# Output projection by seven products on pairs of row blocks, with its weights and first pair prepared inside attention

## The chip, the core and the metric

One core of a Trainium2 chip runs the whole kernel. The metric is device time in microseconds (us); the median of three runs before the change is 849.94 us (849.49 to 851.43).

## What is computed

A gate mixes a Fourier layer and a windowed attention layer, both of the same `x` (2048 rows, 512 columns):

```python
g = _sigmoid((x * gate_w).sum(-1, keepdims=True))
a = x @ dft_hid_re.T;  b = x @ dft_hid_im.T
A = dft_seq_re @ a - dft_seq_im @ b            # 2048 x 2048 matrices
q, k, v = split(x @ wqkv)                       # 32 heads of 16, 256 back
o = softmax(mask(q @ k.T * Dh ** -0.5)) @ v
return g * A + (1 - g) * (o @ wo)
```

(This is cut and reordered from the reference; every matrix is fp32.) The change concerns `o @ wo`, the output projection: 2048 x 512 by 512 x 512, scaled by `1 - g` (`g0` in the kernel) and added to the rest.

## The kernel before, in words

Every product is made of three matmuls: each fp32 operand is split into a rounded part `hi` and a rest `lo`, and `TERMS` lists hi.hi, hi.lo and lo.hi. A split is a cast (`hi`) and a subtraction on DVE (`lo`). So each operand that comes from memory costs a cast and a subtraction before TensorE can use it.

Attention runs over 128 steps (4 groups of heads `g`, 32 blocks of 64 keys). The loop at L864 issues for step `n` the scores `s` (`s_pair`, L366) and, 19 steps later (`LAG`; `k = n - 19`), the transposed scores `t` (`t_pair`, L448), whose exponentials ACT writes to `pt` or `home` (L449) and GpSimd (POOL) masks (L453, L457). Every six steps the products with `v` follow in one run (`pv`, L474), from two value tiles `vpad` that are used in turn. A step needs a "pad" of its queries or keys (`make_pad`, L349 on DVE and L347 on ACT), made one step ahead in one of two buffers. `ring0` and `ring1` hold the queries and keys of a group. A finished piece of `o` is scaled (`o_out`, L495) and stored to `o_scr`.

Between these matmuls `fill` draws dense ones from the generator `dense` (L594), one matmul at a time: the projections, and then the 2048 x 2048 products of the Fourier layer (`c_part`, L528, output `dc`). Their stationary operand comes in pieces (`raw<-ci`, 128 x 1024), loaded two ahead into two buffers and split into one of three `hi`/`lo` buffers: a cast and a subtraction for each half, on DVE (`split_soon`, L115). Each row block of 128 rows takes two pieces of 24 matmuls of 512 columns.

When attention is over, about 8 pieces of the dense work are left. `attention_done` (L779) then reuses `ring0` and `ring1`: it loads `wo` in two halves, splits them on DVE into `fin`, and marks the tail as begun (`FIN`). From then `c_part` calls `tail_step` (L766) at every fourth chunk of three matmuls. A tail step takes up to two row blocks that were prepared three steps before (`wo_block`, L803: 12 matmuls of 512 columns, L811, and one update on DVE, L813), and prepares others (`wo_prep`, L796: a load of `o` from `o_scr`, a cast on ACT and a subtraction on DVE). Row blocks whose Fourier part is finished wait in the list `wait`; blocks 14 and 15 are done ahead of it (`mixed`). The last row block ends the program: `c_final` (L543) makes its last two chunks in two halves of 256 columns (L558), so that the first half is stored (L561) while the second is computed.

The order on TensorE is that of the code. On DVE, ACT, POOL and SP a scheduler orders the instructions by a model of their times when the kernel is built, except where `behind` (L68) holds one after a marked one (`mark`, L64). Nearly all DMAs are issued by SP, in one queue; a DMA that waits there holds those behind it. The tiles `t` and `s` share four PSUM buffers (pool `ps_a`).

Of the kernel before, what the change touches and what calls it, by code (L numbers as in the profile page):

```python
# [7 lines left out]
F32 = mybir.dt.float32  # L8
F32R = mybir.dt.float32r
AF = mybir.ActivationFunctionType  # L10
OP = mybir.AluOpType
# [3 lines left out]
P = 128  # L15
S = 2048
D = 512
DK = D // P
NG = 4
NP = 4  # L20
BQ = 64
NB = S // BQ
WIN = 320
# [4 lines left out]
SWITCH = 6  # L28
# [4 lines left out]
def fnet_window_mix(ctx: ExitStack, tc: tile.TileContext, xT, x, wqk, wv, wr, wi, cr, ci, wo, gw, out):  # L33
    nc = tc.nc

    const = ctx.enter_context(tc.tile_pool(name="const", bufs=1))
# [18 lines left out]
    def ld(dst, src):  # L55
        mark("sp", nc.sync.dma_start(dst, src))  # L56

    def f(ap):
        return ap.bitcast(F32)
# [16 lines left out]
    masks = []  # L76

    def split(hi, lo, raw, act=False):
        if act:
            nc.scalar.copy(hi, raw)  # L80
# [4 lines left out]
        return nc.vector.tensor_sub(lo, raw, f(hi))  # L85
# [251 lines left out]
    def make_pad(i, n):  # L337
        if not 0 <= n < NG * NB:
            return
        t = pads[i][n % NPAD]  # L340
        b = n % NB
        with behind(*(("act", "dve") if n < NPAD else ("dve",) if i == 0 and n < 24 else ())):
            for h in range(2):
                src = f(ring[i][:96, :, b * BQ:(b + 1) * BQ])
                dst = turned(t)[:96, :, :, h] if i else t[:96, :, 64 * h:64 * h + 64]
                if i and h:
                    nc.scalar.activation(dst, src, AF.Copy, scale=half[:96, h:h + 1])  # L347
                else:
                    nc.vector.tensor_scalar(dst, src, half[:96, h:h + 1], None, op0=OP.mult)  # L349
        PAD[i, n] = t  # L350

    ML = {}
# [169 lines left out]

    def c_part(w, chunks, ab, ps, ends):
        for i in chunks:
            if FIN and i % 4 == 0:
                tail_step()
            for n, (a, b) in enumerate(TERMS):
                nc.tensor.matmul(ps, w[a][:, i % 8 * 128:i % 8 * 128 + 128], ab[SC[i]][:, b],  # L528
                                 start=i == ends[0] and a + b == 0, stop=i == ends[1] and a == 1)
                job(i % 8 * 3 + n + 1)  # L530
                if i != chunks[-1] or a == 0:
                    yield
# [10 lines left out]
    def c_final(get, ab):  # L543
        ps = ps_d.tile([P, 512], F32, name="dc", tag="d")
        g = g1[:, 15:16]
        for j in range(2):
            w = get((1, 30 + j))
            yield from c_part(w, range(16)[8 * j:8 * j + 8 - 2 * j], ab, ps, (0, 13))
            yield
        while wait:  # L550
            tail_step()
        r = mixed.pop(15)
        late(nc.vector.scalar_tensor_tensor, r, ps, g, r, OP.mult, OP.add)
        for c, dma in ((slice(0, 256), nc.sync), (slice(256, 512), nc.scalar)):
            ps2 = ps_a.tile([P, 512], F32, name="t", tag="st")
            for i in (14, 15):
                for a, b in TERMS:
                    nc.tensor.matmul(ps2[:, c], w[a][:, i % 8 * 128:i % 8 * 128 + 128], ab[SC[i]][:, b, c],  # L558
                                     start=i == 14 and a + b == 0, stop=i == 15 and a == 1)
            nc.vector.scalar_tensor_tensor(r[:, c], ps2[:, c], g, r[:, c], op0=OP.mult, op1=OP.add)  # L560
            dma.dma_start(out[15][:, c], r[:, c])  # L561
        yield
# [22 lines left out]
    def late(fn, *args):  # L585
        with behind("act", "dve"):
            return fn(*args)  # L587
# [172 lines left out]
    now = []  # L760
    wait = []
    mixed = {}
    born = {}
    clock = iter(range(99))

    def tail_step():  # L766
        t = next(clock)
        for tb in [tb for tb in O if born[tb] < t - 2][:2]:
            if tb in wait:
                wait.remove(tb)  # L770
                ld(out[tb], wo_block(tb, 1))
            else:
                mixed[tb] = wo_block(tb, 0)
        for tb in (*wait[:5], 15, 14, *wait[5:]):
            if tb not in O and tb not in mixed and len(O) < 7 and (tb > now[-1] or tb in wait):
                wo_prep(tb)
                born[tb] = t

    def attention_done():  # L779
        fin = const.tile([P, 8192], F32R, name="fin", tag="ring0")  # L780
        ORAW.extend(f(fin[:, 4112 + 512 * i:4624 + 512 * i]).rearrange("p (g t) -> p g t", g=NG) for i in range(7))
        fin = fin[:, 16:4112].rearrange("p (j c h e) -> p j c h e", j=2, c=2, h=2)
        OS.append(const.tile([P, 8, 2, NG, P], F32R, name="os", tag="ring1"))
        for j in range(2):
            raw = st.tile([P, 1024], F32, name="raw", bufs=2)
# [5 lines left out]
    OS = []  # L791
    ORAW = []
    O = {}
    slot = iter(range(99))

    def wo_prep(tb):  # L796
        oraw = ORAW[0]
        ORAW.append(ORAW.pop(0))
        ld(oraw, o_scr[tb // 4][:, :, tb % 4 * P:tb % 4 * P + P].rearrange("g p t -> p g t"))
        O[tb] = OS[0][:, next(slot) % 8]  # L800
        split(O[tb][:, 0], O[tb][:, 1], oraw[:], True)

    def wo_block(tb, half):  # L803
        o = O.pop(tb)
        r = ev.tile([P, 512], F32, name="ev")
        ld(r, r_scr[half if half or tb < 16 - SWITCH else 2][tb])
        ps = ps_a.tile([P, 512], F32, name="t", tag="st")
        n = 0
        for g in range(NG):
            for a, b in TERMS:  # L810
                nc.tensor.matmul(ps, o[:, a, g], FIN[0][:, g // 2, g % 2, b], start=n == 0, stop=n == 11)  # L811
                n += 1
        nc.vector.scalar_tensor_tensor(r, ps, g0[:, tb:tb + 1], r, op0=OP.mult, op1=OP.add)  # L813
        return r


    stream = dense()
# [39 lines left out]
    def v_next(n):  # L857
        if n < N:
            for c in range(2):
                need(("v", n % NB // 2 + c))  # L860
            with behind(*(("sp",) if n < 8 else ())):
                v_load(n)

    for n in range(N + LAG + 1):  # L864
        k = n - LAG
        if k == 0:
            masks.append(n)
        ring_ahead(n + 1)
        if k in (-1, 4):
            v_spread(0 if k < 0 else 4)  # L870
        if k in (-4, -1, 4):
            v_next({-4: 0, -1: 4, 4: 8}[k])
        if n == 0:
            make_pad(0, 0)
        for p in range(NP):
            if n < N:
                s_pair(n, p)
            fill(n)
            visit = p == 0 and (k - summed >= (6 if more else 4) or k == N)
            if 0 <= k < N and not visit:  # L880
                t_pair(k, p)
            if p == 0:
                make_pad(0, n + 1)
                if k >= -1:
                    make_pad(1, k + 1)
            fill(n)
            if visit:
                for j in range(summed, k):
                    pv(j)
                summed = k  # L890
                if k < N:
                    t_pair(k, p)
            for at_n, at_p, do in TURN if n > 12 else FIRST:
# [61 lines left out]
```

## Time and profile before

| | |
|---|---|
| median of three runs | 849.94 us |
| the profiled execution | 850.96 us |
| its span, first to last instruction | 849.0 us |
| TensorE's granted clock | 1.00 |
| PE busy, 5,166 matmuls | 843.7 us |
| DVE busy | 611.3 us |
| ACT busy | 593.6 us |
| POOL busy | 256.8 us |
| matmuls of the output projection (L811), 512 columns | 192 |

The page gives each engine's busy time and follows the chain of work that ended last. Busy matmuls overlap, so the mean duration of one (392 ns for L811) is not its pace; the pace is the distance between starts. Waits are put down to the instruction that released them. In the profile, "PEld" is the loading of a matmul's stationary operand, and "SPq" the issue of a DMA by SP.

### The profile page before, as it was taken

How to read it: one execution, taken by the hardware profiler on the slowest of the kernel's cores; microseconds unless marked ns; L12 is line 12 of the kernel's file. 1: busy time of each engine (PE TensorE's matmuls, PEld its weight loads, DVE VectorE, ACT ScalarE, POOL GpSimd, SP SyncE). 2: the span in 40 equal slices, each digit the busy share in tenths (PEclk: the TensorE clock that was granted, in tenths of full speed). 3: DMA queues.
4: the chain of work that ended last, by engine and by line, in shares of the span. 5: the costliest groups of instructions: out<-in, count | busy, mean ns of one | idle time of the engine just before them, and what ended most of it. 6: DMA issues, size and time to landing. Idle time of an engine off the chain costs nothing.

```text
span 849.0 us, 16711 instructions
## 1 busy us (share of the span) xinstructions
PE 843.7 (99%) x5166; PEld 691.4 (81%) x5166; DVE 611.3 (72%) x1999; ACT 593.6 (70%) x1798; POOL 256.8 (30%) x578
## 2 busy tenths in 40 slices
PE   9999999999999999999999999999999999999998
PEld 6888888888888788888888887888887878878887
DVE  5588978667978787787787886887987864437531
ACT  6488888878888897787877886877777865532100
POOL 8102332233332233342323333343233364620000
PEclk9999999999999999999999999999999999999999
DMA  8776678476765275533454557969774435339732
GB/s 296 244 228 186 214 243 257 181 233 225 216 222 178 63 211 134 171 115 123 137 158 127 177 150 227 308 216 306 254 215 134 138 121 164 128 118 333 225 134 75
DMA packets 94345, 160.99 MB, mean 190 GB/s; under 512 B 26800, under 2 KB 35760, under 8 KB 94256
## 3 DMA queue, kind: packets, MB, share of 16 engines
q1 hardware_dynamic: 93824, 159.28, 60.2%
q8 instruction: 40, 0.66, 0.3%
q10 hardware_dynamic: 432, 0.66, 0.2%
q14 instruction: 49, 0.40, 0.1%
HBM read 108.27 MB, written 51.64 MB: 188 GB/s over the span
## 4 chain that ended last, share of the span: by engine, by line
PE 94%; DMA 2%; DVE 2%; issue 1%; SPq 0%; ACT 0%; DVEq 0%; ACTq 0%
PE dc L528 39%; PE dqk L280 9%; PE dab L303 9%; PE t L448 9%; PE s L366 8%; PE o L474 8%; PE t L811 5%; PE dv L303 5%; DMA raw<-wo 1%; DMA ev<-l_scr 1%; PE s L268 1%; DVE sm L368 1%; PE dv L592 0%; SPq L56 0%; DVE pad L349 0%
## 5 line engine op out<-in xcount | busy, mean ns | idle before, releaser
L528 PE MATMUL dc<-big,hi 128*128 128x512 f32 x1020 | 344.5, 393 | 0.0
L371 ACT ACTIVATE sm<-sm,ml 128x320 f32<-128x320 f32 (+4 forms) x512 | 277.4, 543 | 59.6 <-DVE ml L368 54.1
L368 DVE CUSTOM_DVE_ANT_0 sm<-s,mask 128x320 f32<-128x320 f32 (+4 forms) x512 | 235.0, 464 | 108.6 <-PE s L366 73.2
L449 ACT ACTIVATE pt<-t 128x320 f32<-128x320 f32 (+4 forms) x392 | 159.8, 411 | 87.7 <-PE t L448 82.1
L528 PE MATMUL dc<-big,lo 128*128 128x512 f32 x510 | 200.3, 393 | 0.0
L528 PEld LDWEIGHTS dc<-big,hi 128*128 128x128 f32 x1020 | 180.4, 188 | 22.6
L448 PE MATMUL t<-ring,pad 128*128 128x320 f32 (+4 forms) x512 | 156.8, 306 | 0.1
L453 POOL TENSOR_SCALAR_AFFINE_SELECT pt<-pt 128x128 f32<-128x128 f32 x196 | 71.2, 363 | 283.3 <-ACT pt L449 279.7
L366 PE MATMUL s<-ring,pad 128*128 128x320 f32 (+4 forms) x512 | 155.3, 303 | 0.3 <-DVE ml L368 0.2
L349 DVE TENSOR_SCALAR pad<-ring,half 96x256 fp32r<-96x256 f32 x384 | 120.4, 360 | 11.9 <-PE t L448 11.7
L448 PEld LDWEIGHTS t<-ring,pad 128*128 128x128 f32 x512 | 96.1, 188 | 31.1 <-issue 8.7
L366 PEld LDWEIGHTS s<-ring,pad 128*128 128x128 f32 x512 | 96.2, 188 | 21.7 <-DVE ml L368 2.0
L528 PEld LDWEIGHTS dc<-big,lo 128*128 128x128 f32 x510 | 95.9, 188 | 11.9
L371 ACT ACTIVATION_READ_ACCUMULATOR sm<-sm,ml 128x1 f32 x512 | 97.4, 190 | 0.0
L587 DVE TENSOR_TENSOR lo<-raw,hi 128x512 fp32r<-128x512 f32 x137 | 93.8, 694 | 0.1
L303 PE MATMUL dab<-hi,big 128*128 128x512 f32 x256 | 89.0, 394 | 0.0
L280 PE MATMUL dqk<-big,hi 128*128 128x512 f32 x240 | 85.0, 393 | 0.0
L431 POOL TENSOR_SCALAR vpad<-vr,half 128x256 f32<-128x256 f32 x64 | 61.3, 969 | 65.3 <-PE o L474 30.3
L587 DVE CAST hi<-raw 128x512 fp32r<-128x512 f32 x137 | 57.7, 431 | 20.5 <-PE dc L528 17.0
L347 ACT ACTIVATE pad<-ring,half 96x256 fp32r<-96x256 f32 x128 | 66.8, 522 | 0.0
L457 POOL TENSOR_SCALAR_AFFINE_SELECT pt<-pt 128x128 f32<-128x128 f32 x172 | 60.8, 354 | 0.0
L474 PE MATMUL o<-pt,vpad 128*32 128x320 f32 (+4 forms) x1072 | 57.7, 351 | 0.0
(96 smaller groups left out, 912.5 us busy)
## 6 DMA issues: line engine op xcount, KB each, us to landing
qk_scr<-home SPq DMA_DIRECT2D x32, 512.0 KB
ring<-qk_scr SPq DMA_DIRECT2D x32, 512.0 KB
raw<-cr SPq DMA_DIRECT2D x32, 512.0 KB
raw<-ci SPq DMA_DIRECT2D x32, 512.0 KB
r_scr<-ev SPq DMA_DIRECT2D x42, 256.0 KB
ev<-r_scr SPq DMA_DIRECT2D x42, 256.0 KB
ab_scr<-home SPq DMA_DIRECT2D x20, 512.0 KB
big<-ab_scr SPq DMA_DIRECT2D x20, 512.0 KB
```

The costliest lines, as they stand in the source:

```text
L280: nc.tensor.matmul(ps, w[a][:, c:c + 128], XT[dk, ss][:, b], start=n == 0, stop=n == 11)
L303: nc.tensor.matmul(ps, XT[dk, ss][:, a, c * 128:(c + 1) * 128], wh[b], start=n == 0, stop=n == 11)
L349: nc.vector.tensor_scalar(dst, src, half[:96, h:h + 1], None, op0=OP.mult)
L366: nc.tensor.matmul(ps[:, :w], PAD[0, n][:, p], ring[1][:, p, k0:k0 + w], start=True, stop=True)
L368: mark("dve", nc.vector.tensor_tensor_reduce(out=sm[:, :w], in0=ps[:, :w], in1=mask[:, WIN - w:], scale=1.0, scalar=3e38, op0=OP.add, op1= ...
L371: mark("act", nc.scalar.activation(sm[:, :w], sm[:, :w], AF.Exp, bias=nm[:, c], scale=-1.0, accum_out=l[:, c]))
L448: nc.tensor.matmul(ps[:, :w], PAD[1, n][:, p], ring[0][:, p, q0:q0 + w], start=True, stop=True)
L449: nc.scalar.activation(pt[:, p, :w], ps[:, :w], AF.Exp, scale=-1.0)
L453: nc.gpsimd.affine_select(a, a, pattern=[[0, 2], [2, 64]], compare_op=OP.is_ge, fill=0.0, base=1, channel_multiplier=-1)
L474: nc.tensor.matmul(OT[g, sb][32 * p:32 * p + 32, q - sb * 512:e - sb * 512], v2[:, p], pt[:, p, q - q0:e - q0], start=first, stop=kb == 8 ...
L528: nc.tensor.matmul(ps, w[a][:, i % 8 * 128:i % 8 * 128 + 128], ab[SC[i]][:, b], start=i == ends[0] and a + b == 0, stop=i == ends[1] and a ...
L587: return fn(*args)
```

## The change

The row blocks are taken in pairs. With a pair's `o` as a matrix of two row blocks by two halves of the contraction (256 each), and `wo` as two halves by two halves of columns, Winograd's form of Strassen's method replaces eight products of quarter size by seven. Each is of 128 rows, 256 deep, 256 columns: two matmuls deep, three terms, six matmuls of 256 columns. It needs four sums of quarters of `o`, four of `wo`, and additions of the results.

- **Weights.** `wo` comes in two column halves into the tiles `pad0` (free after the last scores), in steps 110 and 116. DVE makes four differences of each (`wo_diffs`) and seven casts and seven subtractions (`fin_split`), block by block to step 121, into columns of `ring0` and `ring1` that the last group no longer reads.
- **First pair.** Its `o` is loaded in step 121, summed by DVE in step 123 (`first_sums`), cast by ACT and subtracted by DVE up to step 125. These DVE jobs stand behind the pad that was marked last.
- **Other pairs.** POOL makes the four sums (`wo_sums`), ACT casts and DVE subtracts (`wo_split`); tiles of the attention that has ended (`vpad`, `pad1`, `pad0`, `home`, `pt`) hold the data.
- **Products.** `tail_step` comes twice as often. A pair's first four products (24 matmuls) and the other three (18) are two steps apart, with 12 dense matmuls between; three of the last accumulate on the first ones in PSUM. DVE adds the results to the rows (`into`).
- **Raw pieces.** Behind the end of attention the cast of a dense piece goes to ACT.

```diff
-            jobs.append(lambda c=c: late((nc.vector if masks else nc.gpsimd).tensor_copy, hi[:, c], raw[:, c]))
+            jobs.append(lambda c=c: late(nc.scalar.copy if FIN else (nc.vector if masks else nc.gpsimd).tensor_copy,
+                                         hi[:, c], raw[:, c]))
...
-            if FIN and i % 4 == 0:
+            if FIN and i % 2 == 0:
                 tail_step()
...
-        for tb in [tb for tb in O if born[tb] < t - 2][:2]:
-            if tb in wait:
-                wait.remove(tb)
-                ld(out[tb], wo_block(tb, 1))
...
+        for i, begin in enumerate(BEGIN):
+            if t == begin + 2:
+                wo_end(i)
+            if t == begin:
+                wo_begin(i)
+            if i and t == max(1, begin - 3):
+                wo_split(i)
+            if i and t == max(0, begin - 6):
+                wo_sums(i)
+            if i > 3 and t == begin - 9:
+                wo_load(i)
+
+    BEGIN = range(2, 26, 3)
...
+    def wo_diffs(c):
+        b11, b12, b21, b22 = (q for t in RAW[c] for q in quarters(t, 2))
+        t1, t3, t2, t4 = spare()
+        for t, x, y in ((t1, b12, b11), (t3, b22, b12), (t2, b22, t1), (t4, b21, t2)):
+            nc.vector.tensor_sub(t, x, y)
+        DIFF[c] = b11, b21, b22, t4, t1, t2, t3
+
+    def fin_split(c, m):
+        split(fin(m, 0, c), fin(m, 1, c), DIFF[c][m])
 
     def attention_done():
-        fin = const.tile([P, 8192], F32R, name="fin", tag="ring0")
...
-            ld(raw, wo[j])
-            for c in range(2):
-                split(fin[:, j, c, 0], fin[:, j, c, 1], raw[:, c * 512:c * 512 + 512])
-        FIN.append(fin)
+        RT.append(const.tile([P, 6, 512], F32, name="rt", tag="home"))
...
+        r_load(0)
+        wo_load(1)
+        r_load(1)
+        for i in range(2, 4):
+            wo_load(i)
+        FIN.append(True)
...
+    def sums(eng, s1, s2, s3, s4, a, b):
+        eng.tensor_add(s1, b[:, :256], b[:, 256:])
+        eng.tensor_sub(s3, a[:, :256], b[:, :256])
+        eng.tensor_sub(s2, s1, a[:, :256])
+        eng.tensor_sub(s4, a[:, 256:], s2)
...
+    def wo_split(i):
+        if i > 1:
+            r_load(i)
+        split_a(i)
+        s = EX[i][:, :1024].rearrange("p (m t) -> p m t", m=4)
+        n = 3 if i % 2 else 4
+        split(*halves(spots(1, n, COL[i % 2])), s[:, :n], True)
+        if i % 2:
+            split(*halves(os_spot(6, 1)), s[:, 3], True)
...
+        def product(ps, m, n, start=True):
+            o = os_spot(m, i % 2).rearrange("p (h c t) -> p h c t", h=2, c=2)
+            for c in range(2):
+                for a, b in TERMS:
+                    nc.tensor.matmul(ps, o[:, a, c], fin(n, b, c), start=start and c == 0 and a + b == 0,
+                                     stop=c == 1 and a == 1, skip_group_check=True)
...
+        product(p1, 0, 0)
+        nc.scalar.copy(u, p1)
+        product(p6, 4, 5)
+        nc.vector.tensor_add(u2, p6, u)
+        product(p7, 5, 6)
+        into(r2[:, hi], p7, gb)
+        product(p5, 3, 4)
+        into(r2[:, hi], p5, gb)
+
+        def rest():
+            into(r1[:, hi], u2, ga)
+            product(p1, 1, 1, False)
+            into(r1[:, lo], p1, ga)
+            product(p7, 2, 3, False)
+            into(r2[:, lo], p7, gb)
+            product(p5, 6, 2, False)
+            into(r1[:, hi], p5, ga)
+            into(r2.rearrange("p (n e) -> p n e", n=2), u2.unsqueeze(1).to_broadcast([P, 2, 256]), gb)
...
+    BEFORE_END = {(121, 3): first_load, (123, 0): first_sums, (123, 2): lambda: split_a(0)}
+    for c, k in enumerate((113, 118)):
+        BEFORE_END[(110, 116)[c], 2] = lambda c=c: wo_fetch(c)
+        BEFORE_END[k - 1, 1 + 2 * c] = lambda c=c: wo_diffs(c)
+        for j, m in enumerate((0, 1, 2, 4, 6, 5, 3)):
+            BEFORE_END[k + j // 2, j % 2 * 2] = lambda c=c, m=m: fin_split(c, m)
+    for j, m in enumerate((3, 5, 4, 6)):
+        BEFORE_END[124 + j // 2, j % 2 * 2] = lambda m=m: first_split(m)
```

The change moves instructions on every engine; three places matter. In the rows, `dc` are the dense matmuls, and `ring_267`, `ring_268` are `ring0`, `ring1`; the changed file's lines are one or more higher (L529 for L528).

TensorE between two blocks of the output projection, before:

```order
L811 MATMUL t<-fin,os 128x512 x24
L528 MATMUL dc<-big,hi 128x512 x2
L528 MATMUL dc<-big,lo 128x512
L528 MATMUL dc<-big,hi 128x512 x2
L528 MATMUL dc<-big,lo 128x512
L528 MATMUL dc<-big,hi 128x512 x2
L528 MATMUL dc<-big,lo 128x512
L528 MATMUL dc<-big,hi 128x512 x2
L528 MATMUL dc<-big,lo 128x512
L811 MATMUL t<-fin,os 128x512 x24
```

and TensorE at the second half of the first pair and the first half of the second, in the change:

```order
L529 MATMUL dc<-big,lo 128x512
L922 MATMUL t<-ring_267 128x256 x12
L922 MATMUL t<-ring_267,ring_268 128x256 x6
L529 MATMUL dc<-big,hi 128x512 x2
L529 MATMUL dc<-big,lo 128x512
L529 MATMUL dc<-big,hi 128x512 x2
L529 MATMUL dc<-big,lo 128x512
L922 MATMUL t<-ring_267 128x256 x6
L922 MATMUL t<-ring_268 128x256 x18
```

Where 24 matmuls of 512 columns stood for two row blocks, 24 and 18 of 256 columns stand now, with 12 dense ones between the halves of a pair and 6 between pairs.

ACT at the end of attention (`pt<-t` are the exponentials of the last two steps), before:

```order
L347 ACTIVATE pad_0_265<-ring_268,half 96x256
L449 ACTIVATE pt<-t 128x192 x4
L347 ACTIVATE pad_1_266<-ring_268,half 96x256
L449 ACTIVATE pt<-t 128x128 x4
L449 ACTIVATE pt<-t 128x64 x4
L80 CAST os<-fin 128x512 x16
```

and in the change:

```order
L348 ACTIVATE pad_1_266<-ring_268,half 96x256
L450 ACTIVATE pt<-t 128x128 x2
L80 CAST ring_267<-oraw 128x2x256
L588 CAST hi<-raw 128x512
L450 ACTIVATE pt<-t 128x128 x2
L450 ACTIVATE pt<-t 128x64 x4
L588 CAST hi<-raw 128x512 x2
L80 CAST ring_267<-oraw 128x256
L80 CAST ring_268<-pt 128x3x256
```

A cast of the second pair's first block (`oraw`) and a cast of a dense piece now stand ahead of the last six exponentials.

SP's queue over the last steps of attention (`o_scr` holds the finished `o`, `rt` the rows to be added to), before:

```order
L56 DMA r_scr_10_203<-ev 128x512
L56 DMA raw<-ci 128x1024 x2
L56 DMA r_scr_11_204<-ev 128x512
L56 DMA ev<-l_scr_172 128x1x512
L56 DMA ev<-r_scr_12_221 128x512
L56 DMA raw<-wo 128x1024
```

and in the change:

```order
L56 DMA r_scr_10_203<-ev 128x512
L56 DMA raw<-ci 128x1024
L56 DMA oraw<-o_scr_174 128x4x128 x2
L56 DMA raw<-ci 128x1024
L56 DMA oraw<-o_scr_173 128x4x128
L56 DMA rt<-r_scr_0_193 128x512
L56 DMA rt<-r_scr_1_194 128x512
L56 DMA r_scr_11_204<-ev 128x512
L56 DMA ev<-l_scr_172 128x1x512
```

Loads of `o` for the fourth pair and of the second pair's first block, and of rows, have come in ahead of the store `r_scr_11`; the loads of `wo` have left this place for steps 110 and 116.

More of the change, by code (lines that the diff above doesn't have):

```diff
@@ L348, in make_pad @@
                 else:
[L349 removed]
+                    mark(f"pad{i}", nc.vector.tensor_scalar(dst, src, half[:96, h:h + 1], None, op0=OP.mult))
         PAD[i, n] = t
@@ L549, in c_final @@
             yield
-        while wait:
+        while O:
             tail_step()
@@ L792, in fnet_window_mix @@
+    RT = []
     ORAW = []
     O = {}
[L794 to L814, printed above, removed]
+    R = {}
@@ new lines, in fnet_window_mix, with wo_load, first_load @@
+    EX = {}
+    def wo_load(i):
+        pair = [15, 14] if i == 2 else [wait.pop(0) for _ in range(2)]
+        raw = []
+        for tb in pair:
+            raw.append(ORAW.pop(0))
+            ORAW.append(raw[-1])
+            ld(raw[-1].rearrange("p (g t) -> p g t", g=NG),
+               o_scr[tb // 4][:, :, tb % 4 * P:tb % 4 * P + P].rearrange("g p t -> p g t"))
+        O[i] = pair, raw
+    def first_load():
+        ORAW.extend(const.tile([P, 512], F32, name="oraw", tag=f"pad0_{b}")[:] for b in range(2))
+        wo_load(0)
@@ new lines, in r_load, with extra @@
+    def r_load(i):
+        k = 4 if i == 2 else i % 2 * 2
+        R[i] = RT[0][:, k], RT[0][:, k + 1]
+        for tb, t in zip(O[i][0], R[i]):
+            with behind("sp"):
+                ld(t, r_scr[2 if i == 2 else 1][tb])
+    def sums(eng, s1, s2, s3, s4, a, b):
[3 more added lines that the diff above has]
+        eng.tensor_sub(s4, a[:, 256:], s2)
+    def extra(i):
+        EX[i] = at.tile([P, NP, WIN], F32, name="pt", bufs=4).rearrange("p a b -> p (a b)")
+        return EX[i]
@@ new lines, in wo_sums, with first_sums, split_a, first_split @@
+    def wo_sums(i):
+        e = extra(i)
+        sums(nc.gpsimd, *(e[:, 256 * k:256 * k + 256] for k in range(4)), *O[i][1])
+    def first_sums():
+        EX[0] = spare()
+        sums(nc.vector, *EX[0], *O[0][1])
+    def split_a(i):
+        a, b = O[i][1]
+        split(*halves(spots(0, 2, COL[i % 2])), a.rearrange("p (m t) -> p m t", m=2), True)
+        split(*halves(os_spot(2, i % 2)), b[:, 256:], True)
+    def first_split(m):
+        split(*halves(os_spot(m, 0)), EX[0][m - 3], True)
@@ new lines, in wo_split, with wo_begin, into @@
+    def wo_split(i):
[7 more added lines that the diff above has]
+            split(*halves(os_spot(6, 1)), s[:, 3], True)
+    def wo_begin(i):
+        pair = O[i][0]
+        r1, r2 = R[i]
+        ga, gb = (g0[:, tb:tb + 1] for tb in pair)
+        lo, hi = slice(0, 256), slice(256, 512)
+        p1, p6, p7, p5 = (ps_a.tile([P, 512], F32, name="t", tag="st")[:, lo] for _ in range(4))
+        def product(ps, m, n, start=True):
[4 more added lines that the diff above has]
+                                     stop=c == 1 and a == 1, skip_group_check=True)
+        def into(r, t, g):
+            nc.vector.scalar_tensor_tensor(r, t, g, r, op0=OP.mult, op1=OP.add)
+        e = EX[i] if i else extra(i)
+        u, u2 = e[:, 1024:1280], e[:, :256]
+        product(p1, 0, 0)
[15 more added lines that the diff above has]
+            into(r2.rearrange("p (n e) -> p n e", n=2), u2.unsqueeze(1).to_broadcast([P, 2, 256]), gb)
+            for tb, r in zip(pair, (r1, r2)):
+                if i == 2:
+                    mixed[tb] = r
+                else:
+                    ld(out[tb], r)
+        O[i] = rest
```

56 lines of the change are left out of this document (43 added, 13 removed).

## The prediction

> **What bounds the kernel now.** I read the engines and the chain of waits first.
>
> ```profile
> PE 843.7 (99%) x5166; PEld 691.4 (81%) x5166; DVE 611.3 (72%) x1999; ACT 593.6 (70%) x1798; POOL 256.8 (30%) x578
> PE 94%; DMA 2%; DVE 2%; issue 1%; SPq 0%; ACT 0%; DVEq 0%; ACTq 0%
> ```
>
> TensorE has work in 843.7 of 849.0 us and holds 94% of the chain. A busy PE may still be a slow PE, so the next view is the windows from the end of attention on: the stretch with both DMA steps of the chain, the stretch with the output projection, and the last one.
>
> ```profile
> 759.31:775.90 16.59, 16.48 (x87) 13.00 (x85) 9.62 (x19) 3.55 (x7) 0.49 (x2) 1.00 0.98 299
> 775.90:837.59 61.69, 61.69 (x270) 50.78 (x271) 27.31 (x45) 6.54 (x11) 0.00 (x0) 1.00 0.60 193
> 837.59:845.83 8.24, 8.23 (x43) 6.86 (x41) 1.99 (x3) 0.00 (x0) 0.00 (x0) 1.00 0.08 32
> ```
>
> The columns are PE, weight loads, DVE, ACT, POOL, granted clock, DMA share, GB/s. PE lacks 0.11 us in the first stretch and nothing afterwards, at clock 1.00. The DMA steps on the chain (the loads of wo) therefore cost PE almost nothing: dense matmuls run under them. Moving the preparation of wo earlier buys about 0.1 us by itself; the gain must come from fewer PE columns.
>
> **Term 1, the matmuls.** The chain gives their pace, the group their count, the timeline the pace of 256 columns (the only such run without other matmuls between, in the last block).
>
> ```profile
> L811 PE MATMUL t<-fin,os 128*128 128x512 f32 x192 | 45.5, 392 | 0.1
> 791.03 5.49 PE t L811 x24
> 796.52 2.72 PE dc L528 x12
> 844.23 0.40 PE L558 MATMUL t<-big,hi 128*128 128x256 f32 x2
> 844.82 0.31 PEld L558 LDWEIGHTS t<-big,hi 128*128 128x128 f32 x2
> 845.54 0.28 PE L558 MATMUL t<-big,lo 128*128 128x256 f32 x1
> ```
>
> Removed: 192 matmuls at 5.49/24 = 0.2288 us, 43.9 us. Added: 8 pairs x 7 products x 6 = 336 matmuls of 256 columns (24 in the first half of a pair, 18 in the second). From the first to the twelfth of the 256-column run are 11 steps in 845.54 - 844.23 = 1.31 us, 0.119 us each: 336 x 0.119 = 40.0 us. The term is **-3.9 us**. Its good end is half the pace of 512, 0.1144 us: 38.4 us, -5.5. Its bad end is a weight load that does not overlap: a single load lasts 0.188 us (the row shows two in 0.31), 336 x 0.188 = 63.2 us, +19.3. I take 0.119, since those rows have a load for each matmul too and the pace held for all twelve.
>
> The Trainium skill (TensorE: Matmul & The Clock Gate, The mechanism) speaks against the change: a weight load overlaps a running matmul only where the two use different row groups. All of these use all 128 rows; with loads serial, more and shorter matmuls would lose. The two loads in 0.31 us, at a step of 0.119, do not bear it out for this form.
>
> **Term 2, waits on PE.**
>
> ```profile
> L811 PEldq EVENT_SEMAPHORE  x11: 51/51/51, 770.0 to 830.6; - x11
> ```
>
> The order has 45 waiting places in the products for 19 in the old blocks. A run of 24 takes 5.49 us where two dense rows of 12 take 5.44: 0.05 us a run, 0.4 in 8 runs, for 19 waits 0.02 each. The 26 more cost 0.5 at that rate, at most 26 x 0.051 = 1.3 us, and nothing where the queue is ahead; I take **+0.4**, a little under the rate, since a part of the 0.05 may have another cause.
>
> **Term 3, DVE in the last attention blocks.** Eight differences, 14 casts, 14 subtractions, and the first pair's sums and splits stand in DVE's queue between the pads of attention.
>
> ```profile
> 699.00:751.20 52.20, 52.20 (x381) 42.72 (x380) 23.36 (x49) 28.61 (x69) 26.41 (x61) 1.00 0.45 148
> 8.90 0.41 DVE L163 TENSOR_TENSOR lo<-pt,hi 128x256 fp32r<-128x256 f32 x1
> 9.24 0.68 DVE L85 TENSOR_TENSOR big<-pt,big 128x512 fp32r<-128x512 f32 x1
> 769.62 3.09 DVE L85 TENSOR_TENSOR os<-fin,os 128x512 fp32r<-128x512 f32 x5
> 772.63 0.74 DVE L742 SCALAR_TENSOR_TENSOR ev<-dc,g,ev 128x512 f32<-128x512 f32 x1
> ```
>
> Start to start, 256 columns take 9.24 - 8.90 = 0.34 us, 512 take 3.01/5 = 0.60. 31 operations of 256 columns (8 + 14 + 4 sums + 5 splits) are 10.5 us, one of 512 0.6, 14 casts at most 0.34 each 4.8: 15.9 us. With the 23.4 there, DVE is at 39.3 of 52.2 us, 75%. Behind a late one stand the pads that PE's t matmuls need; a pad is made a block ahead. I take **0**. Without that cover every us that DVE falls behind is one of PE.
>
> **Term 4, the hand-over.** The cast of pair 1's first block stands in ACT's queue ahead of the last six exponentials. Its data comes by SP's queue, into a tile that the PV matmuls free.
>
> ```profile
> 742.81 6.13 SPq L56 DMA_DIRECT2D raw<-ci  x2
> 753.56 1.15 PE L474 MATMUL o<-home,vpad 128*32 128x320 f32 x16
> 755.39 0.56 ACT L449 ACTIVATE pt<-t 128x128 f32<-128x128 f32 x2 [3.80 <-PE t L448]
> 757.68 0.33 SPq L56 DMA_DIRECT2D r_scr<-ev  x1
> 759.43 0.19 PE L448 MATMUL t<-ring,pad 128*128 128x64 f32 x1
> 761.32 5.00 SPq L56 DMA_DIRECT2D fin<-o_scr  x5
> 767.55 0.62 ACT L80 CAST os<-fin 128x512 fp32r<-128x512 f32 x1 [6.86 <-DMA fin<-o_scr]
> 750.00:760.00 10.00, 10.00 (x83) 7.03 (x82) 3.10 (x6) 2.86 (x10) 1.66 (x4) 1.00 0.22 80
> 271.25 3.96 DMA ev<-l_scr
> ```
>
> The older value tile is free in the middle of the home run, about 754.0; SP is idle then between 748.9 and 757.7. Such a load took 6.2 us (761.32 to 767.55) with the DMA engines at 0.98, another of 256 KB 3.96 us; here the share is 0.22, so I take 4: it lands at 758.0. ACT then casts (0.62), casts a half piece (0.62) and runs an exponential (0.28): 759.5. Two exponentials stand ahead of the cast, so of four PSUM tiles two are free, and the first matmul that must wait is that of 759.43. The term is the landing + 1.5 - 759.4: 0.1 us, with semaphores **+0.3**; by 6.2 us it is +2.3; nothing is its good end.
>
> **Term 5, DVE, ACT and POOL behind the pairs.** Per pair DVE has seven updates of 256 columns, one of 512, and splits of 1,792 columns.
>
> ```profile
> 780.65 0.74 DVE L813 SCALAR_TENSOR_TENSOR ev<-t,g,ev 128x512 f32<-128x512 f32 x1
> 781.32 1.28 DVE L85 TENSOR_TENSOR os<-fin,os 128x512 fp32r<-128x512 f32 x2
> L80 ACT CAST os<-fin x16: 615/621/626, 767.6 to 804.5; 128x512 fp32r<-128x512 f32 x16
> L587 POOL TENSOR_TENSOR lo<-raw,hi x5: 1295/1302/1430, 68.0 to 88.2; 128x512 fp32r<-128x512 f32 x5
> L457 POOL TENSOR_SCALAR_AFFINE_SELECT pt<-pt x172: 286/293/962, 102.6 to 742.2; 128x128 f32<-128x128 f32 x172
> ```
>
> An update of 512 takes 0.67 us start to start; less 0.26 (0.60 - 0.34) one of 256 takes 0.41. So 7 x 0.41 + 0.67 = 3.5; splits 0.60 + 0.34 + 1.12 = 2.1; the raw pieces' subtractions 2 x 0.60 x 18/24 = 0.9; a share of the evictions 0.25: 6.8 us. PE's period is 18 dense matmuls at 2.72/12, 4.1, and 42 x 0.119, 5.0: 9.1 us. DVE is at 75% and its updates have a dense stretch of 2.7 us before PE needs the tile again. ACT has some four casts and a copy, 1,792 columns at 0.62 per 512 or less, 2.2, plus 0.9 for pieces, under 4 of 9.1. I take **0**; with that cover gone, see the first rival.
>
> **Term 6, the end.**
>
> ```profile
> 838.41 0.33 SPq L56 DMA_DIRECT2D out<-ev  x1
> 845.79 0.33 SPq L561 DMA_DIRECT2D out<-ev  x1
> SPq L56 <- DMA out<-ev: 18.4, 11, 2.8
> ```
>
> Before, the last full block leaves 7.4 us ahead of the last store. Now pair 7's two blocks leave some 1.5 to 2 us ahead of it, and a store takes up to 2.8 us. Between nothing and 0.8 I take **+0.3**.
>
> **Sum:** -3.9 + 0.4 + 0 + 0.3 + 0 + 0.3 = -2.9 us. The profiled execution (span 849.0, time 850.96, 1.96 around it) lies 1.0 above the median of 849.94; from 850.96 the sum gives 848.1, from the median **847.0 us**, the forecast.
>
> **Rivals.** *DVE becomes the bound.* The select of 0.293 us that took 0.962 is 0.669 longer, one DVE subtraction: POOL and DVE hold each other up at times. POOL now makes four sums a pair, each about half of 1.30, 2.6 us. If each held DVE for its whole length, DVE would need 9.4 us for 9.1: +0.3 x 8 = 2.4, 849.4 us. Against it: subtractions ran beside POOL in all of attention with a median of 0.685.
>
> The Trainium skill (SBUF — State Buffer, Who interferes with whom) states this as a lock: a DVE instruction with two SBUF inputs and a GpSimd one that reads SBUF exclude each other. The 0.962 agrees; but some 4 of the 6.8 us have two SBUF inputs.
>
> *The hand-over by the slow load.* Landing at 760.2 costs 2.3 instead of 0.3: 849.0.
>
> *SP holds the hand-over.* Pairs count from 0. The loads of pair 3 stand ahead of pair 1's and wait for the first pair's splits to free their tiles. If they, or a late store, hold SP until the 757.68 of the profile, the load lands at 757.7 + 6.2 = 763.9 and PE loses 763.9 + 1.5 - 759.4 = 6.0: 852.7, slower. It cancels the gain from a landing at 761.1 and is slower by 0.2% from 762.8.
>
> *Loads do not overlap* in the products: -3.9 becomes +19.3, 870 us. The twelve of L558 speak against it.
>
> **Chances.** This kernel's time can be told from no change from about 0.2%, 1.7 us: faster is below 848.2, slower above 851.6. Forecast 0.63 (faster); DVE bound 0.13 and slow load 0.06 (both same); SP held 0.14 and loads 0.04 (slower). The forecast's own range is 844.9 (849.94 less 5.5, with 0.5 for the rest) to 848.2; with the others 844.5 to 852.5.
>
> **What would show it.** Right: products of 24 in 2.86 us and 18 in 2.14, PE without a gap after 767, DVE near 75% there, POOL's sums at 0.65. Term 4 shows as a wait of the exponentials on o's load about 756 to 758. Wrong: PE idle before a product until DVE; updates well over 0.41 us; weight loads that follow one another; a last store that lands much later behind the product's end.

## The result, and the profile after

Device microseconds; the ratio is that of the changed kernel to the kernel before, with its 95% interval.

| kernel | median (lowest to highest), runs | kernel before beside it | ratio |
|---|---|---|---|
| changed, the runs of the comparison | 848.49 (846.26 to 852.16), 22 | 850.08 (849.49 to 853.13), 22 | 0.9979 [0.9969, 0.9989] |
| changed, first repeat | 847.43 (846.63 to 848.06), 5 | 850.76 (849.29 to 852.35), 14 | 0.9959 [0.9946, 0.9971] |
| changed, second repeat | 847.21 (846.23 to 849.64), 6 | 849.66 (848.59 to 851.63), 12 | 0.9968 [0.9955, 0.9980] |

The change makes the kernel faster, by 0.2 to 0.4%. The forecast was 847.0 us, a ratio of 0.9966: inside the intervals of both repeats, just outside that of the first set, whose ratio, taken from the 849.94 us of the forecast, gives 848.2 us, the edge of the forecast's range. The profiled execution took 846.26 us, with a span of 844.4. First its engines and its chain of waits by engine:

```profile
PE 839.5 (99%) x5310; PEld 695.9 (82%) x5310; DVE 644.3 (76%) x2083; ACT 609.0 (72%) x1832; POOL 295.0 (35%) x606
PE 99%; DVE 1%; issue 0%; ACT 0%; DVEq 0%; ACTq 0%
```

TensorE has 4.2 us less work in 144 more matmuls (192 of 512 columns are gone, 336 of 256 are there), and the two loads of wo have left the chain. Next the pieces of the chain from the first pair on (start, length, engine, what, how many):

```profile
766.13 2.87 PE t L922 x24
769.00 2.75 PE dc L529 x12
771.75 2.15 PE t L922 x18
773.90 1.39 PE dc L529 x6
775.29 2.87 PE t L922 x24
778.16 2.75 PE dc L529 x12
780.91 2.36 PE t L922 x18
783.27 1.39 PE dc L529 x6
784.66 2.95 PE t L922 x24
```

A pair is 24 matmuls of products, 12 dense ones, 18 of products, 6 dense ones. The forecast was 2.86 and 2.14 us for the products; 2.87 and 2.15 stand there. Two pieces are longer, by 0.21 (2.36) and by 0.08 (2.95): these are the only waits of TensorE in the eight pairs of this execution.

The windows of the same kernel (PE, weight loads, DVE, ACT, POOL, granted clock, DMA share, GB/s): the last attention blocks, then the first pair, the pairs after it, and the late pairs.

```profile
699.00:751.20 52.20, 52.20 (x385) 42.22 (x387) 36.63 (x91) 29.82 (x74) 35.72 (x62) 1.00 0.54 177
767.10:775.90 8.80, 8.80 (x59) 8.05 (x59) 6.91 (x12) 3.67 (x7) 6.78 (x9) 1.00 0.54 161
775.90:800.00 24.10, 24.10 (x157) 21.93 (x157) 21.50 (x37) 9.13 (x16) 15.02 (x15) 1.00 0.71 229
800.00:833.00 33.00, 33.00 (x222) 30.50 (x222) 22.24 (x46) 8.42 (x16) 3.15 (x4) 1.00 0.36 120
```

TensorE is full in all four, at clock 1.00. DVE rises in the attention blocks from 23.4 to 36.6 us of 52.2. In the tail it is 89% busy from 776 to 800 (21.50 of 24.10), where POOL works too, and 67% later (22.24 of 33.00).

### The profile page after: what moved, and what is told of

The parts are those of the page before. It is cut to its first block, busy times and chain, and to the rows that moved or that the text cites. A ratio compares the mean times of both kernels' runs of the same rounds, so it can differ in the third digit from the quotient of the medians.

```text
span 844.4 us, 17173 instructions
## 1 busy us (share of the span) xinstructions
PE 839.5 (99%) x5310; PEld 695.9 (82%) x5310; DVE 644.3 (76%) x2083; ACT 609.0 (72%) x1832; POOL 295.0 (35%) x606
## 4 chain that ended last, share of the span: by engine, by line
PE 99%; DVE 1%; issue 0%; ACT 0%; DVEq 0%; ACTq 0%
PE dc L529 42%; PE dab L304 10%; PE dqk L281 10%; PE t L449 9%; PE s L367 8%; PE o L475 8%; PE dv L304 5%; PE t L922 5%; PE s L269 1%; PE dv L593 0%; PE s L387 0%; DVE pad L350 0%; PE t L559 0%; DVE sm L369 0%; ACT sm L372 0%
## 5 line engine op out<-in xcount | busy, mean ns | idle before, releaser
L529 PE MATMUL dc<-big,hi 128*128 128x512 f32 x1020 | 344.6, 393 | 0.0
L529 PE MATMUL dc<-big,lo 128*128 128x512 f32 x510 | 200.2, 393 | 0.0
L529 PEld LDWEIGHTS dc<-big,hi 128*128 128x128 f32 x1020 | 179.4, 188 | 21.4
L454 POOL TENSOR_SCALAR_AFFINE_SELECT pt<-pt 128x128 f32<-128x128 f32 x196 | 73.9, 377 | 277.1 <-ACT pt L450 276.0
L529 PEld LDWEIGHTS dc<-big,lo 128*128 128x128 f32 x510 | 95.9, 188 | 12.0
L588 DVE TENSOR_TENSOR lo<-raw,hi 128x512 fp32r<-128x512 f32 x137 | 94.8, 700 | 2.8 <-ACT hi L588 2.0
L588 DVE CAST hi<-raw 128x512 fp32r<-128x512 f32 x126 | 54.5, 439 | 13.3 <-PE dc L529 11.4
L454 POOL TENSOR_SCALAR_AFFINE_SELECT home<-home 128x128 f32<-128x128 f32 x60 | 32.6, 544 | 89.6 <-ACT home L450 86.6
L458 POOL TENSOR_SCALAR_AFFINE_SELECT pt<-pt 128x128 f32<-128x128 f32 x172 | 63.2, 368 | 0.0
```

The lines of the kernel that those rows point to most:

```text
L454: nc.gpsimd.affine_select(a, a, pattern=[[0, 2], [2, 64]], compare_op=OP.is_ge, fill=0.0, base=1, channel_multiplier=-1)
```

## The tail, measured from event to event

Single executions of one kernel differ by 3 us and more, as much as the change is worth, so spans don't compare well. The tail does: from the first matmul of the last long PV run to the end of the last matmul. Here are these first matmuls in the kernel before and in its repeat:

```profile
751.92 1.82 PE L474 MATMUL o<-pt,vpad 128*32 128x320 f32 x24
```

```profile
751.11 1.82 PE L474 MATMUL o<-pt,vpad 128*32 128x320 f32 x24
```

and the first and the last in the changed kernel:

```profile
750.68 1.82 PE L475 MATMUL o<-pt,vpad 128*32 128x320 f32 x24
840.85 0.28 PE L559 MATMUL t<-big,lo 128*128 128x256 f32 x1
```

The tail of the kernel before is 845.82 - 751.92 = 93.90 us and in its repeat 844.58 - 751.11 = 93.47; of the changed kernel 841.13 - 750.68 = 90.45, and in its three repeats 90.59, 90.61 and 90.93. The means are 93.7 and 90.6: the tail is 3.0 us shorter. The terms of the forecast that lie in it (1, 2 and 4) add up to 3.2; term 6 lies behind the last matmul.

The repeat of the kernel before has no wait in its tail, so its chain gives the clean comparison; the kernel before had lost 0.4 us in its first product run (5.90 us instead of 5.49), which waited for the split of the second half of wo, loaded late:

```profile
PEld t L811 <- DVE fin L85: 0.5, 1, 0.5
```

The pieces of the repeat are:

```profile
761.31 12.05 PE dc L528 x52
773.36 5.49 PE t L811 x24
778.85 2.72 PE dc L528 x12
836.35 6.80 PE dc L528 x30
```

- Products: 8 x 5.49 = 43.92 us before; 8 x (2.87 + 2.15) = 40.16 after, and 0.29 of waits: **-3.47**.
- Dense matmuls: 166 in both tails. Before, 12.05 + 7 x 2.72 + 6.80 = 37.89. After, 22 in 5.25, then eight times 12 in 2.75 and 6 in 1.39: 38.37. **+0.48**, which is 0.03 for each of 16 dense runs that follow a run of products (0.45 without the rounding of the pieces).
- From the PV run to the end of attention's last matmuls: 761.31 - 751.18 = 10.13 before and 760.88 - 750.75 = 10.13 after (chain times): **0**.

Together -2.99, or -3.02 without rounding; the tails of these two profiles differ by 93.47 - 90.45 = 3.02. Against the first profile of the kernel before the tail is 3.45 shorter, since the early preparation of wo also takes that 0.4 away.

## The experiments

Eight runs in two groups, each group on one chip with the kernel before beside it.

**The change again, and the kernel before again.** No edit. The question was how much of a difference between two profiles belongs to the change.

> The changed kernel once more, for a second profile and its time beside the variants. In its first profile (span 844.4 us) PE stood still for only 0.3 us behind the end of attention, though its median is some 2 us above that execution. Theory A (hand-over): in slower executions the load of pair 1's first block lands later than the 756.2 us of that profile, the last exponentials wait behind ACT's cast, and PE has a gap of 1 to 3 us at the last t matmuls. Theory B (DVE and POOL in the tail): the gap stands before products (0.2 us at 780.9 in the first profile), 1 to 3 us in sum. Theory C: the difference lies in attention ahead of step 110, as in the kernel before, and the stretch behind step 110 takes the same time within 0.3 us in every profile.

> A third profile of the changed kernel, read for the same gaps: A has them at 757 to 760 us, B before products, C nowhere behind step 110.

> The changed kernel again, beside the next three. In three profiles so far the stretch from the start of the last long PV run to the last matmul took 90.4 to 90.6 us, the kernel before 93.84 us in its one profile, while the PV run itself began anywhere between 750.8 and 752.2 us. Theory C (what differs between executions lies ahead of that point): this stretch is again within 90.3 to 90.7 us, and the ratio to the kernel before is 0.996. If the tail itself varies, a stretch over 91.5 us turns up.

> The kernel before once more, for a second profile. Theory C: 93.7 to 94.0 us from the start of the last long PV run to the last matmul, so that the gain of the tail is 3.3 us in any pair of executions. If the first profile of the kernel before was a slow one in its tail, under 93 us.

Measured: 847.43 us in the first, a single execution of 847.35 in the second, 847.21 in the third; a single one of the kernel before took 849.58 beside a median of 849.66. Two expectations missed: one tail of the changed kernel is 90.93 us where 90.7 was the upper bound, and the repeat of the kernel before has 93.47 where 93.7 was the lower one, so that the clean gain is 3.0 us and not 3.3. The changed kernel's executions part ahead of the change. The profile of the second repeat proper (849.64 us, 2.4 above the median of its group) reaches the last PV run 2.83 us later than the first profile, and its tail is only 0.48 longer. Its row of the PV run and its wait of DVE in the same execution (engine, line, what is waited for: us, times, longest):

```profile
753.51 1.82 PE L475 MATMUL o<-pt,vpad 128*32 128x320 f32 x24
DVE ev L496 <- DMA ev<-l_scr: 2.6, 1, 2.6
```

The same operation waits in every profile: 1.3 us in the first profile of the kernel before, and 1.0 in the first of the changed kernel, where the wait is put down to a matmul:

```profile
DVE ev L495 <- DMA ev<-l_scr: 1.3, 1, 1.3
DVE ev L496 <- PE dab L304: 1.0, 1, 1.0
```

It ends near 275 us, over 400 us ahead of the first load of wo that the change moved. In all ten profiles, TensorE's stretch between the PV runs around it (from about 272 to about 293 us) is longer by what this wait is longer: 1.52 us in the execution above, whose wait is 2.57 instead of 1.05 us. The other 1.31 us of its 2.83 were lost in smaller pieces, 0.60 ahead of this stretch and 0.71 behind it. So this one load makes about half of that delay, in code that both kernels share.

The tails themselves differ only by TensorE's waits in the products. These are 0.29, 0.44, 0.44 and 0.78 us in the four profiles of the changed kernel, and each tail less its waits is 90.15 or 90.16 us.

**The hand-over: is the cast in ACT's queue in the way?**

```
-        nc.scalar.activation(pt[:, p, :w], ps[:, :w], AF.Exp, scale=-1.0)
+        mark("exp", nc.scalar.activation(pt[:, p, :w], ps[:, :w], AF.Exp, scale=-1.0))
...
-        split_a(i)
+        with behind("exp"):
+            split_a(i)
```

> ACT's cast of pair 1's first block stands behind the last exponentials instead of ahead of six of them; nothing else moves. Theory A: the median falls by 0.5 to 2 us below the changed kernel's and its spread of 6 us shrinks to the 3.6 us of the kernel before. B and C: the same time within 0.5 us, since the wait of 1.5 us that ACT has there in the first profile delays no matmul.

Measured: 846.79 us (846.62 to 848.08), ratio 0.9958 [0.9945, 0.9970], beside 0.9959 for the unedited kernel in the same group; its tail is 90.64 us beside 90.59. No difference. What the cast costs in the changed kernel is seen on ACT and on SP's queue:

```profile
756.20 0.62 ACT L80 CAST ring<-oraw 128x512 fp32r<-128x512 f32 x1 [1.49 <-DMA oraw<-o_scr]
756.73 0.61 ACT L588 CAST hi<-raw 128x512 fp32r<-128x512 f32 x1
757.25 0.66 ACT L450 ACTIVATE pt<-t 128x128 f32<-128x128 f32 x4
```

```profile
753.10 0.36 SPq L56 DMA_DIRECT2D oraw<-o_scr  x1
```

The load is issued at 753.10 and ACT starts on its data at 756.20. ACT waits 1.49 us and then runs four exponentials in one piece, and TensorE, which has free PSUM tiles and dense matmuls, loses nothing: the 10.13 us above.

**Who makes the sums: POOL, DVE or nobody.** The first edit moves the four sums of the later pairs from POOL to DVE, the second puts one memset in their place.

```
-        sums(nc.gpsimd, *(e[:, 256 * k:256 * k + 256] for k in range(4)), *O[i][1])
+        sums(nc.vector, *(e[:, 256 * k:256 * k + 256] for k in range(4)), *O[i][1])
```

```
-        sums(nc.gpsimd, *(e[:, 256 * k:256 * k + 256] for k in range(4)), *O[i][1])
+        nc.gpsimd.memset(e[:, :1024], 0.0)
```

> The four sums of each later pair on DVE instead of POOL. Theory B in the form that POOL and DVE hold each other up: DVE's subtraction of 1,024 columns falls from 1.82 us back to about 1.12 and the gaps before products vanish, time 0 to 1 us lower; DVE's own work rises by 4 x 0.34 = 1.4 us a pair, to 8.2 of 9.1 us. If DVE's load alone decides, the time is 1 to 4 us higher, with PE waiting for DVE before products. A and C: within 0.5 us.

> POOL's four sums of each later pair are left out: one memset of the four quarters stands for them, so the products of these quarters are of zeros. If POOL's reading sums hold DVE up, DVE's subtraction of 1,024 columns falls from 1.82 to about 1.2 us, that of 768 from 1.10 to 0.95, and the waits of 0.3 us before products vanish: 0.3 us less. If DVE is merely late by its own load, these durations stay.

Measured: on DVE 849.19 us (848.30 to 852.06), ratio 0.9984 [0.9973, 0.9995], 1.8 above the changed kernel in its group; without sums 846.73 (846.25 to 847.99), ratio 0.9965 [0.9953, 0.9977], 0.5 below the changed kernel in its group, within the intervals of the two.

The groups of DVE in the tail (busy us, mean ns of one, idle time before) show what POOL does to it. The changed kernel:

```profile
L926 DVE SCALAR_TENSOR_TENSOR rt<-t,g,rt 128x256 f32<-128x256 f32 x40 | 19.0, 478 | 9.3 <-PE t L922 8.8
L926 DVE SCALAR_TENSOR_TENSOR rt<-pt,g,rt 128x256 f32<-128x256 f32 x8 | 4.8, 603 | 0.1
L85 DVE TENSOR_TENSOR ring<-pt,ring 128x1024 fp32r<-128x1024 f32 x3 | 4.3, 1419 | 0.6 <-ACT ring L80 0.6
```

and without sums:

```profile
L926 DVE SCALAR_TENSOR_TENSOR rt<-t,g,rt 128x256 f32<-128x256 f32 x40 | 19.2, 480 | 11.3 <-PE t L922 10.7
L926 DVE SCALAR_TENSOR_TENSOR rt<-pt,g,rt 128x256 f32<-128x256 f32 x8 | 3.8, 480 | 0.1
L85 DVE TENSOR_TENSOR ring<-pt,ring 128x1024 fp32r<-128x1024 f32 x3 | 3.7, 1217 | 0.0
```

The updates that read PSUM (t) take 478 and 480 ns: POOL does not touch them. The same operation with pt in place of t goes from 480 to 603, the subtraction of 1,024 columns from 1,217 to 1,419, though with two of the changed kernel's repeats at 1,264 and 1,263 it varies. These means mix short and long ones: of the eight updates with pt two take 943 and 953 ns, the others 475 to 506. POOL pays too; its sums in the changed kernel, and the select that met DVE's first pair:

```profile
L877 POOL TENSOR_TENSOR pt<-oraw 128x256 f32<-128x256 f32 x7 | 8.2, 1165 | 0.0
L876 POOL TENSOR_TENSOR pt<-oraw 128x256 f32<-128x256 f32 x7 | 6.2, 882 | 20.4 <-DVE rt L926 8.7 <-DMA oraw<-o_scr 7.8 <-issue 3.9
```

```profile
767.21 0.74 POOL L878 TENSOR_TENSOR pt<-pt,oraw 128x256 f32<-128x256 f32 x1
742.14 3.06 POOL L454 TENSOR_SCALAR_AFFINE_SELECT home<-home 128x128 f32<-128x128 f32 x1 [0.46 <-ACT home L450]
```

A sum that meets nobody takes 0.74 us (DVE is idle from 766.7 to 768.9); the means are 0.88 to 1.17. So each engine slows the other, and a meeting need not cost both: at 795.8 us a sum takes 1.91 us beside two of DVE's subtractions of 512 columns, which keep their 681 and 684 ns. What TensorE pays is the sum of its waits for DVE, here those of its weight loads in the changed kernel and with the sums on DVE:

```profile
PEld t L922 <- DVE rt L926: 0.2, 1, 0.2
```

```profile
PEld t L922 <- DVE rt L926: 2.2, 2, 1.3
```

Without sums there is no such row and all sixteen runs of products last 2.87 or 2.15 us. Without sums the tail is 90.52 us, no shorter, because the memset comes early: ACT's casts of what it wrote stand ahead of the last exponentials, whose select the last PV matmuls need. From the PV run to the dense restart are 762.01 - 751.49 = 10.52 us instead of 10.13. Less that 0.39, the tail is 90.13, about the 90.16 of the changed kernel without its waits. The sums thus cost TensorE 0.29 to 0.78 us. As expected, DVE's subtractions of 1,024 and 768 columns are back at 1,217 and 955 ns, and the waits are gone.

That the mutual hold-up alone makes these waits is not shown. The wait comes when a subtraction of 1,024 columns stands in DVE's queue ahead of an update. In the first profile of the changed kernel (TensorE loses 0.29) it took long; in the second repeat proper (0.78) it took less, but waited longer for ACT's cast of POOL's sums, which came later behind a later load of o:

```profile
778.43 1.82 DVE L85 TENSOR_TENSOR ring<-pt,ring 128x1024 fp32r<-128x1024 f32 x1 [0.57 <-ACT ring L80]
782.21 1.36 DVE L85 TENSOR_TENSOR ring<-pt,ring 128x1024 fp32r<-128x1024 f32 x1 [1.72 <-ACT ring L80]
```

The memset neither reads nor waits for that load, so the run without sums takes both causes away at once.

With the sums on DVE the loss has a place, the second half of the first pair:

```profile
774.54 0.98 PE L922 MATMUL t<-ring 128*128 128x256 f32 x6 [0.64 <-DVE rt L926]
776.66 0.98 PE L922 MATMUL t<-ring,ring 128*128 128x256 f32 x6 [1.14 <-DVE rt L926]
```

```profile
767.10:775.90 8.80, 7.78 (x51) 6.80 (x49) 7.52 (x19) 3.77 (x8) 0.00 (x0) 1.00 0.62 189
775.90:800.00 24.10, 23.34 (x156) 21.60 (x157) 22.57 (x48) 8.49 (x15) 0.00 (x0) 1.00 0.73 229
800.00:833.00 33.00, 33.00 (x215) 30.17 (x214) 25.79 (x54) 8.88 (x16) 0.00 (x0) 1.00 0.33 112
```

Twice the products wait for a PSUM tile, which is free only after an update that stands behind the sums of later pairs in DVE's queue; ahead of these sums DVE itself had waited 0.81 us for their load. The tail is 92.43 us, 2.0 longer. From 800 on DVE has 25.79 of 33.00 us and TensorE waits no more. Each of the two expectations met a part: DVE's operations fell back (the update to 479 ns, the subtraction of 1,024 columns to 1,215), and yet the time rose, since DVE had the sums to make. So POOL is the better place for the sums while their pairs are being handed over.

**The staging without Strassen.** Eight plain products of quarters instead of seven, no differences and no sums, four quarters split for each pair and for each half of wo; the preparation in attention's last blocks stays.

```
-        product(p1, 0, 0)
-        nc.scalar.copy(u, p1)
-        product(p6, 4, 5)
...
+        product(p1, 0, 0)
+        product(p1, 1, 1, False)
+        into(r1[:, lo], p1, ga)
+        product(p6, 0, 3)
+        product(p6, 1, 2, False)
+        into(r1[:, hi], p6, ga)
```

> The same staging, places and pairs, but eight plain products a pair instead of seven: no differences of wo, no sums of o, four quarters to split instead of seven, 384 matmuls of 256 columns. Theory 1 (the gain is the number of columns): PE needs 48 x 0.1195 = 5.7 us more, less 0.3 of waits that go: 5.4 us above the changed kernel and about 2 us above the kernel before. Theory 2 (a good part of the gain is that weights and first pair are prepared inside attention): no more than 3 us above the changed kernel, not above the kernel before.

Measured: 852.87 us (852.43 to 853.76), ratio 1.0038 [1.0026, 1.0050]: 5.7 us above the changed kernel in its group, 3.2 above the kernel before, where the theory of the columns expected 5.4 and about 2. Its chain:

```profile
766.97 2.87 PE t L912 x24
769.85 2.75 PE dc L529 x12
772.59 2.87 PE t L912 x24
775.47 1.39 PE dc L529 x6
```

Its tail is 95.92 us, 2.45 more than the clean tail before. Both parts are in the rows: products 16 x 2.87 = 45.92 for 43.92, +2.00, and the dense runs of 12 and 6 at 2.75 and 1.39, +0.48: +2.48. The early preparation of weights and first pair thus brings no time of its own against a tail without waits; with the same columns in matmuls half as wide it loses. The gain of the change is the eighth product that is left out: 8 pairs x 6 x 0.1195 = 5.7 us.

No variant is clearly faster than the changed kernel.

## Why the prediction was right, and where its sizes were off

**The bound, and term 1 with term 2.** The bound and term 1 are right. TensorE stayed full, and the columns decided, as the staging without Strassen shows. Forecast were 40.0 us of products and 0.4 of waits; the products take 40.16 and the waits in them 0.29, so the two terms together are -3.5 as forecast.

The working of term 2 was wrong, and its size came near by luck. It took the 0.05 us by which a run of 24 products is longer than dense rows as a price of waits. The starts of the single matmuls show something else: in the old runs every group of three takes 229, 232 and 226 ns, in dense rows 227, 227 and 226. That is regular, in 64 groups for 19 waiting places. The new runs go at a steady 120 ns but where TensorE waits for DVE, which is the matter of term 5.

The forecast also lacked a term: each dense run behind products is 0.03 us longer than before, 0.48 us in all. Its first five starts are 234, 236, 228, 232 and 231 ns apart, then 227 as before. It shows in every kernel with halves, that without sums and that with eight products too, so it hangs neither on waits for DVE nor on Strassen. What makes it was not tried.

One reading under the bound was too low: the late loads of wo cost TensorE not 0.1 but 0.4 us in the profile that the forecast read. The window's busy time hid it, since the ends of matmuls are modelled; the starts show it.

**The loads of weights.** The rival with loads that do not overlap fell. The group of loads of the changed kernel is:

```profile
L922 PEld LDWEIGHTS t<-ring 128*128 128x128 f32 x312 | 39.7, 191 | 1.5 <-DVE rt L926 0.2
```

Each lasts 191 ns and the matmuls still start every 0.1195 us (2.87/24): 312 loads fill only 39.7 us, so they overlap even one another. The rule of the Trainium skill (TensorE: Matmul & The Clock Gate, The mechanism) that a load overlaps a matmul only where the two use different row groups is not borne out here: all rows are used by both. What the same section allows besides, a load ahead of time into a background buffer, would fit these rows, but no run here shows what the loads went into.

**Term 3.** Right at 0: from the PV run that starts at 704.07 in the changed kernel to that at 750.75 are 46.68 us, and from 705.32 to 751.99 in the kernel before 46.67. DVE had 36.6 us there, less than the 39.3 of the forecast.

**Term 4.** The mechanism was right, a wait of ACT on pair 1's load, and the price too high: 0 instead of +0.3. ACT had the load 3.1 us after its issue instead of 4, and was done with the four exponentials behind the cast at 757.91, 7.2 us after the PV run's start, where the forecast had the first matmul that must wait at 7.5. The last two exponentials then waited for TensorE and not the other way round. SP did not hold it: the rival that would have made the kernel slower did not occur.

**Term 5 and the first rival.** The total of 0 was nearly right (0.29 us, in the repeats up to 0.78), the working was not. DVE was put at 75% throughout and POOL's sums at 0.65 us. DVE is at 89% from 776 to 800, since POOL makes the sums of several pairs there one after another and operations of DVE with two SBUF inputs get longer beside it; without the sums it is at 77% (18.54 of 24.10 us). A sum takes 0.74 us alone and 0.88 to 1.17 on the mean. The forecast left out the order of the queue: a split that waits for its data holds the updates behind it, whatever DVE's share. The first rival thus described a part of what happens, and its price (2.4 us) failed because it laid the hold-up evenly on all eight pairs. In the profiles of the changed kernel TensorE waits in the second and third pair only; from 800 on DVE is at 67%. The experiment with the sums on DVE shows that the cover there is thin: 2.2 us of waits.

**Term 6.** Off: +0.3 was taken, 0.1 at most measured. The forecast went by the last store of SP; the last of all is issued by ACT, before and after:

```profile
846.37 0.35 ACTq L561 DMA_DIRECT2D out<-ev  x1
841.68 0.35 ACTq L562 DMA_DIRECT2D out<-rt  x1
```

From its issue to the end of the span are 2.6 us before (849.0) and 2.7 after (844.4); from the last matmul's end, 3.2 and 3.2. The two stores ahead of it do not delay it.

**The sum.** Measured: -3.47 in place of -3.5, +0.48 that was not forecast, 0 for the +0.3 of term 4, 0 to 0.1 for the +0.3 of term 6: about -3.0 for -2.9. The mechanism was right, but that the sum fits this closely is luck: the missing term and the two that were too high cancel.

**What stays open.** The repeats give -3.3 and -2.5 us and the comparison -1.6, at the same code. In the comparison 16 of 22 runs are above 848 us, in the two repeats 3 of 11. The late load near 275 us makes an execution up to 1.5 us longer in these profiles, and smaller losses add to it; more of both in the comparison would explain its median. Only profiled executions show them, so this is argued and not shown. What the whole kernel gains is thus known to 1.6 to 3.3 us, what its tail gains to 3.0 (3.45 where the load of wo came late). The waits of 0.29 to 0.78 us in the products have two possible causes that no run parts.

## What to carry to other kernels

When TensorE is full, count the columns that a change removes and price them at the pace of that very shape; then add 0.03 us for each run of wide matmuls that follows narrow ones. Preparing operands earlier is worth only the time that the bound engine lost to them before, here 0.4 us in one profile and nothing in the other. For the added vector work look at the window where the helpers overlap and at what stands ahead of it in their queues, not at their mean share. Where one execution differs from the next by as much as the change, compare the stretch between two events that both kernels have.

## What the runs showed of the hardware

- DVE operations with two SBUF inputs get longer beside POOL's sums (480 to 603 ns, 684 to 768 for the subtraction of 512 columns at L588) and POOL's sums beside DVE (0.74 to 1.17 us, a select of 0.29 up to 3.06); DVE operations with one PSUM input do not (478 and 480 ns). This agrees with the lock that the Trainium skill describes (SBUF — State Buffer, Who interferes with whom). The mean price differs from group to group, since not every operation meets a sum and at a meeting sometimes POOL alone pays: 26% (updates of 256 columns), 12% (L588), 1% (updates of 512 columns, 746 to 755 ns).
- A run of 512-column matmuls costs 0.03 us more after 256-column ones than after 512-column ones, for 6 and for 12 alike (1.39 and 2.75 us; 12 took 2.72 before). The surplus lies in its first five matmuls (234, 236, 228, 232 and 231 ns from start to start, then 227).
- Weight loads of 128 x 128 overlap matmuls on all 128 rows and one another: 191 ns each in the trace, at a step of 0.1195 us.
